# Attention and gated MLP on one core: the split of the attention output interleaved bank by bank, the second pair's split moved ahead of the weight steps, and ten weight blocks in the attention

## The chip, the core and the metric

The kernel runs on one core of a Trainium2 chip. A core has engines that run side by side, each taking its own instructions in order: TensorE (PE in the profile; its weight loads are shown apart as PEld), VectorE (DVE), ScalarE (ACT), GpSimd (POOL), and SyncE (SP), which here only issues transfers between the chip's memory and the core's on-chip memory, SBUF. TensorE writes its results to a small accumulator memory, PSUM, from which ScalarE and VectorE read them. The metric is the device time of one execution in microseconds (us), lower being better. An engine that needs another's result waits at a semaphore, and everything behind the waiting instruction on that engine waits with it.

## What is computed

Two stages, in fp32: attention with a sigmoid in place of the softmax over 12 heads, and a gated MLP over its output, with a normalisation and a mixing of positions in the gate. Cut to what matters:

```python
# q, k, v: (8, 12, 448, 64)
scores = q @ k.T / sqrt(64) - log(448)
x = concat_heads(sigmoid(scores) @ v)             # (8, 448, 768)
h = relu(x @ w_in)                                # w_in (768, 1024)
u, v = h[..., :512], h[..., 512:]
v_n = (v - mean(v)) / sqrt(var(v) + 1e-6)
v_s = einsum('ts,bsd->btd', w_spatial, v_n) + b_spatial
out = (u * v_s) @ w_out                           # w_out (512, 768)
```

## The kernel before, in words

**Products in three terms.** TensorE multiplies numbers in a rounded form (`F32R`). To keep fp32 accuracy, an operand is split into a high part (the rounded copy) and a low part (the operand less that copy); a product is the sum of high·high, low·high and high·low (`TERMS`). The helper `split` (L97 to L99) makes both parts: a copy on a chosen engine into the high part, then a `tensor_sub` on VectorE into the low part.

**Stages.** The eight batch entries go in four groups `m` of two. Each group has two stages. In the *attention* a loop runs over six pairs of units (`attention`, L484); a unit is two heads of one entry. Then come the *gate and output* products: `gate_values` (pv), `spatial` (pg), `gated` (pu) and `output` (po).

**One turn of the attention.** A turn writes seven score tiles psc (first the short one, L251, then the even unit's three and the odd unit's three, L269), ScalarE makes `at` from each with the sigmoid (L277), and TensorE multiplies them with v into `pav` (L295). `pav` is one tile of two PSUM banks: bank 0 for the even unit, bank 1 for the odd one. It is split into the two parts of `x_s`: ScalarE casts bank 0 and bank 1 (L305), then VectorE subtracts for bank 0 and bank 1 (L307). The very first turn takes its scores from the raw q and k; all later turns use `qks`, the split q and k. The cast of `qks` is ScalarE's in the first two entries, which are group 0 (`b > 1` in L237 otherwise), and VectorE's later.

**PSUM.** All PSUM tiles come from one ring of four buffers of two banks each (`banks`, tag ps2). One turn takes eight: the short tile, three even, three odd, and `pav`. So the fourth tile of a turn, psc of t = 2, stands in the buffer of the previous turn's `pav` and has to wait until all four reads of it are done; and a turn's `pav` stands in the buffer of its own psc of t = 2, and has to wait until ScalarE has made `at` from that.

**Weights.** w_in, w_spatial and w_out come from memory in 22 blocks and are split on the way by the generator `weight_steps`, which is advanced by `load_weights`. The first `NFIRST` = 11 blocks (the v half of w_in, w_spatial, and one block of the u half) take three advances each, or one for w_spatial, on VectorE alone, during group 0's attention: `weigh` spends `NYIELDS` = 25 of them there, four in a turn and five in the last. The other 11 take two advances each, with part of the work on ScalarE, during group 0's gate stage; a block's parts are spread over three rounds (`begin`; `middle`; the subtraction).

**What sets the order.** Each engine runs its instructions in the order in which the code issues them (`in_program_order`); the framework puts in the semaphore waits. It treats the reads of one PSUM tile by two engines as dependent: the later reader waits for the earlier.

Of the kernel before, what the change touches and what calls it, by code (L numbers as in the profile page):

```python
# [8 lines left out]
F32 = mybir.dt.float32  # L9
# [26 lines left out]
def attn_gmlp_kernel(  # L36
# [25 lines left out]
    nc = tc.nc  # L62
    B, NHP, _, _ = qk.shape
    S = out.shape[3]
    D = P // 2
    NCC = out.shape[1]
    DM = NCC * P
    F = w_in.shape[1] // (4 * NCC)
    NFC = F // P
# [18 lines left out]
    x_s = const.tile([P, 2, NCC, 2 * S], F32R, name="x_s")  # L88
# [8 lines left out]
    def split(hi, lo, src, copy):  # L97
        copy(hi, src)  # L98
        nc.vector.tensor_sub(lo, src, hi.bitcast(F32))  # L99

    def banks(name):
        return ps_2.tile([P, 2, 512], F32, tag="ps2", name=name)


    WEIGH = 4
# [22 lines left out]
    def weight_steps():  # L128
# [8 lines left out]
        def load(n):  # L137
            if n < len(steps):
                src, _, i = steps[n]
                w = 512 if src is w_sp else 1024  # L140

                if n < NFIRST:
                    raw = work.tile([P, 1024], U32, tag="tmp", name=f"wraw_{n}", bufs=3)[:, :w]
                else:
                    raw = work.tile([P, 1024], U32, tag="raw", name=f"wraw_{n}", bufs=4)
                raws[n] = raw.bitcast(F32) if src is w_sp else raw
                nc.sync.dma_start(raws[n], src[:, i * w : (i + 1) * w])
# [10 lines left out]

        for n, (src, dst, i) in enumerate(steps[:NFIRST]):
            load(n + AHEAD)  # L160
# [35 lines left out]
        begun, joined = {}, {}  # L196
        for n in range(NFIRST, len(steps) + 2):
            load(n + AHEAD)
# [8 lines left out]
            yield  # L207


    NFIRST = NCC + NFC + 1  # L210
    NYIELDS = 3 * (NCC + 1) + NFC

    weights = weight_steps()

    def load_weights(n):
        for _ in range(n):
            next(weights, None)
# [16 lines left out]
    def attention_splits(b, hp):  # L234
        raw = loaded[b, hp][:, :PART]
        s = work.tile([P, 2, 2 * S], F32R, tag="split", name=f"qks_{b}_{hp}", bufs=3)[:, :, :PART]
        split(s[:, 0], s[:, 1], raw, nc.vector.tensor_copy if b > 1 else nc.scalar.copy)  # L237
        parts_of[b, hp] = s
# [5 lines left out]
    def attention_scores(b, hp, t):  # L244
        psc = banks(f"psc_{b}_{hp}_{t}")
        if t == NFULL:
            for odd in range(2):
                raw = loaded[b, hp + odd]
                for j in range(2):
                    rows = slice(j * D, (j + 1) * D)  # L250
                    nc.tensor.matmul(  # L251
                        psc[odd * HALF : (odd + 1) * HALF, j, :S],
                        raw[rows, PART:],
                        raw[rows, FULL:PART],
                        start=True,
                        stop=True,
                    )
        else:
            unit = b, hp + t // (NFULL + 1)
            k = t % (NFULL + 1) * P  # L260
            if unit in parts_of:
                s = parts_of[unit]
                ops = [(s[:, a], s[:, e]) for a, e in TERMS]
            else:
                ops = [(loaded[unit], loaded[unit])]
            for i, (st, mv) in enumerate(ops):
                for j in range(2):
                    rows = slice(j * D, (j + 1) * D)
                    nc.tensor.matmul(  # L269
                        psc[:, j, :S],  # L270
                        st[rows, k : k + P],
                        mv[rows, FULL:PART],
                        start=i == 0,
                        stop=i == len(ops) - 1,
                    )
        at = work.tile([P, 2, 512], F32, tag="big", name=f"at_{b}_{hp}_{t}", bufs=BIG)[:, :, :S]
        nc.scalar.activation(at, psc[:, :, :S], AF.Sigmoid, bias=bias_s, scale=QK)  # L277
        return at

    def attention_values(b, hp, ats):  # L280
        vt = values[b, hp]
        pav = banks(f"pav_{b}_{hp}")
        evens, odds = range(NFULL), range(NFULL + 1, TILES)
        for t in (*evens, *odds, NFULL):
            at = ats(t)
            for odd in range(2):
                if t == NFULL:
                    rows = slice(odd * HALF, (odd + 1) * HALF)
                elif (t > NFULL) == odd:
                    rows = slice(0, P)  # L290
                else:
                    continue
                for j in range(2):
                    heads = slice(j * D, (j + 1) * D)
                    nc.tensor.matmul(  # L295
                        pav[heads, odd, :S],
                        vt[rows, t, heads],
                        at[rows, j],
                        start=t == odd * (NFULL + 1),
                        stop=t == NFULL,  # L300
                    )
        cols = slice((b % 2) * S, (b % 2 + 1) * S)
        parts = [(x_s[:, :, hp + odd, cols], pav[:, odd, :S]) for odd in range(2)]
        for x, ps in parts:
            nc.scalar.copy(x[:, 0], ps)  # L305
        for x, ps in parts:
            nc.vector.tensor_sub(x[:, 1], ps, x[:, 0].bitcast(F32))  # L307

    def product(ps, pairs, more=(), start=True, stop=True):

        ops = [(st(a), mv(c)) for st, mv in pairs for a, c in TERMS] + list(more)
        for i, (st, mv) in enumerate(ops):
            nc.tensor.matmul(ps, st, mv, start=start and i == 0, stop=stop and i == len(ops) - 1)  # L313
# [10 lines left out]
    def half_of(w, o, k, n):  # L324

        block, col = divmod((o // 2 * n + k) * 2 + o % 2, 4)
        return w[:, block, :, col * P : (col + 1) * P]
# [84 lines left out]
    def gated(b, fcs, copy=nc.scalar.copy):  # L412

        odd = b % 2
        g = gates.pop((b, fcs))
        pu = banks(f"pu_{b}_{fcs[0]}")
        for i, fc in enumerate(fcs):
            fs = slice(fc * P, (fc + 1) * P)
            product(
                pu[:, i, :S],  # L420
                [
                    (
                        lambda a, cc=cc: half_of(w_in_s, fc, cc, NCC)[:, a],
                        lambda c, cc=cc: x_s[:, c, cc, odd * S : (odd + 1) * S],
                    )
                    for cc in range(NCC)
                ],
            )
        load_weights(2)
        nc.vector.scalar_tensor_tensor(g, pu[:, :, :S], 0.0, g, op0=ALU.max, op1=ALU.mult)  # L430
        gs = work.tile([P, 2, 2 * S], F32R, tag="split", name=f"gs_{b}_{fcs[0]}", bufs=3)
        gs = gs.rearrange("p a (i s) -> p a i s", i=2)
        split(gs[:, 0], gs[:, 1], g, copy)
        for i, fc in enumerate(fcs):
            hidden[b, fc] = gs[:, :, i]
        load_weights(1)

    def output(b, es, parts=1, final=False):

# [32 lines left out]
    def ahead(f, n, end=len(units)):  # L472
        if n < end:
            f(*units[n])
# [9 lines left out]
    def attention(m):  # L484

        first, end = 2 * NHP * m, 2 * NHP * (m + 1)
        ats = {}
        budget = [NYIELDS if m == 0 else 0]

        def weigh(n):  # L490
            n = min(n, budget[0])
            budget[0] -= n
            load_weights(n)

        def scores(n, ts):
            for t in ts:
                ats[n, t] = attention_scores(*units[n], t)

        short, evens, odds = (NFULL,), tuple(range(NFULL)), tuple(range(NFULL + 1, TILES))
        for n in range(first, end, 2):  # L500
            if n:
                scores(n, short + evens)
            else:
                scores(n, evens)

            def loads():
                ahead(value_loads, n + 2, end)
                ahead(attention_loads, n + 4, end)
                ahead(attention_loads, n + 5, end)

            if n and n == first:
                yield
                attention_splits(*units[n + 1])
            if n:
                loads()
            scores(n, odds)
            if not n:
                scores(n, short)
            weigh(WEIGH + (n + 2 == end))
            if not n:  # L520
                loads()
            ahead(attention_splits, n + 2, end)
            ahead(attention_splits, n + 3, end)
            attention_values(*units[n], lambda t: ats.pop((n, t)))

    start_loads(0)
    load_weights(1)
    warm_up()
    pairs = [(0, 1), (2, 3)]
    running = attention(0)  # L530
    for m in range(B // 2):
        for _ in running:
# [80 lines left out]
```

## Time and profile before

| what | value |
|---|---|
| median of three runs | 690.48 us (690.3 to 690.51) |
| the profiled execution's own time | 690.91 us |
| its span, first to last instruction | 689.1 us |
| PE busy | 677.9 us, 98% |
| DVE busy | 280.6 us, 41% |
| ACT busy | 245.8 us, 36% |
| granted TensorE clock | 1.000 |

The span is 1.81 us shorter than the time of the execution it comes from. The page gives busy time by engine and the costliest groups of instructions; the chain of work that ended last follows the end of the program back to its start, at each step to what released it; the waits list who sat idle for whom; the timeline lists single instructions in order of time. A busy PE is not a PE at its peak, since the ends of matmuls are modelled.

### The profile page before, as it was taken

To read this page: it belongs to the slowest core of one execution; us is meant where nothing else is said; L and a number is where in the kernel's file an instruction comes from. 1 tells how busy PE (TensorE), PEld (TensorE's weight loads), DVE (VectorE), ACT (ScalarE), POOL (GpSimd) and SP (SyncE) were. 2 spreads that over 40 slices of the span, in tenths; PEclk is the share of its full clock that TensorE was granted. 3 is DMA by queue.
4 is the path that set the end of the run, shared out by engine and by line. 5 is a ranking of instruction groups with operands and counts; after the bars stand their busy time and mean duration, and the time that the engine had idled before them with its cause. 6 is when DMAs were issued, how large, how long until landed. Compare 5 with 4: busy or idle time off the path is not lost.

```text
span 689.1 us, 9062 instructions
## 1 busy us (share of the span) xinstructions
PE 677.9 (98%) x3826; PEld 508.2 (74%) x3826; DVE 280.6 (41%) x447; ACT 245.8 (36%) x303; POOL 18.5 (3%) x36
## 2 busy tenths in 40 slices
PE   8999999999999999999999999999999999999997
PEld 3545789998655488999864558899985546889996
DVE  3868688823234037222242414621233421653020
ACT  6777322313467510011356741011136664101111
POOL 0000010000000001000000001100000000110000
PEclk9999999999999999999999999999999999999999
DMA  6854113060433000005062200000515410000102
GB/s 235 321 183 156 49 44 95 28 214 25 166 131 107 1 1 0 1 28 186 28 212 88 104 1 0 1 1 27 187 54 187 138 51 1 0 1 0 54 28 80
DMA packets 20553, 55.37 MB, mean 80 GB/s; under 512 B 1953, under 2 KB 8353, under 8 KB 20513
## 3 DMA queue, kind: packets, MB, share of 16 engines
q1 hardware_dynamic: 20224, 54.57, 22.7%
q8 instruction: 30, 0.49, 0.3%
q10 hardware_dynamic: 288, 0.23, 0.1%
q14 instruction: 11, 0.08, 0.0%
HBM read 43.78 MB, written 11.01 MB: 80 GB/s over the span
## 4 chain that ended last, share of the span: by engine, by line
PE 92%; DVE 4%; ACT 3%; issue 1%
PE pav L295 20%; PE pu L313 17%; PE po L313 17%; PE pv L313 17%; PE pg L313 10%; PE psc L269 10%; DVE x_s L307 3%; ACT x_s L305 3%; PE psc L251 1%; PE warm L322 0%; DVE qks L99 0%; DVE gs L99 0%; DVE g L430 0%; DVE osb L463 0%; ACT osb L461 0%
## 5 line engine op out<-in xcount | busy, mean ns | idle before, releaser
L277 ACT ACTIVATE at<-psc,bias_s 128x896 f32<-128x896 f32 x168 | 154.3, 1032 | 23.0 <-PE psc L251 18.6
L295 PE MATMUL pav<-at,v 128*64 128x448 f32 (+1 forms) x768 | 135.4, 548 | 0.0
L313 PE MATMUL po<-gs,w_out_s 128*128 128x448 f32 x576 | 120.4, 368 | 1.0 <-DVE osb L463 0.9
L313 PE MATMUL pu<-x_s,w_in_s 128*128 128x448 f32 x576 | 118.0, 365 | 0.0
L313 PEld LDWEIGHTS po<-gs,w_out_s 128*128 128x128 f32 x576 | 107.7, 188 | 12.6 <-DVE osb L463 1.2
L313 PE MATMUL pv<-w_in_s,x_s 128*128 128x512 f32 x504 | 115.5, 390 | 0.0
L313 PEld LDWEIGHTS pu<-x_s,w_in_s 128*128 128x128 f32 x576 | 108.2, 188 | 8.5
L313 PEld LDWEIGHTS pv<-w_in_s,x_s 128*128 128x128 f32 x504 | 94.3, 188 | 22.3 <-issue 2.8
L295 PEld LDWEIGHTS pav<-at,v 128*64 128x64 f32 (+1 forms) x768 | 44.2, 135 | 80.5 <-issue 73.3
L269 PE MATMUL psc<-qks 64*128 64x448 f32 x828 | 96.8, 374 | 5.6 <-DVE x_s L307 4.6
L269 PEld LDWEIGHTS psc<-qks 64*128 64x128 f32 x828 | 77.8, 184 | 31.9 <-PE psc L269 11.6
L307 DVE TENSOR_TENSOR x_s<-pav,x_s 128x448 fp32r<-128x448 f32 x48 | 27.8, 620 | 135.8 <-ACT x_s L305 135.8
L313 PE MATMUL pg<-w_sp_s,vn 128*128 128x448 f32 x352 | 72.8, 365 | 0.0
L313 PEld LDWEIGHTS pg<-w_sp_s,vn 128*128 128x128 f32 x352 | 66.0, 187 | 5.8
L467 ACT COPY osb<-po 128x896 f32<-128x896 f32 x23 | 20.9, 908 | 114.9 <-PE po L313 104.6
L430 DVE SCALAR_TENSOR_TENSOR g<-pu,g 128x896 f32<-128x896 f32 x16 | 17.5, 1091 | 82.5 <-PE pu L313 82.5
L98 DVE CAST qks<-raw 128x832 fp32r<-128x832 f32 x36 | 21.2, 588 | 72.1 <-DMA raw<-qk_dram 36.9
L305 ACT CAST x_s<-pav 128x448 fp32r<-128x448 f32 x48 | 23.2, 536 | 76.0 <-PE pav L295 76.0
L99 DVE TENSOR_TENSOR qks<-raw,qks 128x832 fp32r<-128x832 f32 x46 | 46.7, 1025 | 4.5 <-ACT qks L98 1.4
L98 ACT CAST gs<-g 128x896 fp32r<-128x896 f32 x12 | 11.3, 943 | 100.7 <-DVE g L430 100.7
L348 ACT ACTIVATE rv<-pv 128x1024 f32<-128x1024 f32 (+1 forms) x16 | 14.7, 916 | 76.0 <-PE pv L313 74.3
L352 DVE BATCH_NORM_STATS2 stats<-rv 128x6 f32<-128x512 f32 x28 | 19.0, 679 | 39.5 <-ACT rv L348 39.5
(42 smaller groups left out, 242.5 us busy)
## 6 DMA issues: line engine op xcount, KB each, us to landing
raw<-qk_dram SPq DMA_DIRECT2D x48, 448.0 KB, 5.3
v<-v_dram SPq DMA_DIRECT2D x24, 448.0 KB, 3.4
out_dram<-osb SPq DMA_DIRECT2D x23, 448.0 KB, 2.6
wraw<-w_in_dram SPq DMA_DIRECT2D x12, 512.0 KB, 5.8
wraw<-w_out_dram SPq DMA_DIRECT2D x6, 512.0 KB, 3.6
wraw<-w_sp_dram SPq DMA_DIRECT2D x4, 256.0 KB, 5.1
b_bc<-b_sp_dram SPq DMA_DIRECT2D x1, 256.0 KB, 5.0
out_dram<-osb ACTq DMA_DIRECT2D x2, 112.0 KB, 1.7
```

The source lines that it names most:

```text
L98: copy(hi, src)
L99: nc.vector.tensor_sub(lo, src, hi.bitcast(F32))
L269: nc.tensor.matmul(psc[:, j, :S], st[rows, k : k + P], mv[rows, FULL:PART], start=i == 0, stop=i == len(ops) - 1,)
L277: nc.scalar.activation(at, psc[:, :, :S], AF.Sigmoid, bias=bias_s, scale=QK)
L295: nc.tensor.matmul(pav[heads, odd, :S], vt[rows, t, heads], at[rows, j], start=t == odd * (NFULL + 1), stop=t == NFULL,)
L305: nc.scalar.copy(x[:, 0], ps)
L307: nc.vector.tensor_sub(x[:, 1], ps, x[:, 0].bitcast(F32))
L313: nc.tensor.matmul(ps, st, mv, start=start and i == 0, stop=stop and i == len(ops) - 1)
L348: nc.scalar.activation(rv[:, :n], pv[:, :n], AF.Relu)
L352: nc.vector.bn_stats(stats, rv[:, i])
L430: nc.vector.scalar_tensor_tensor(g, pu[:, :, :S], 0.0, g, op0=ALU.max, op1=ALU.mult)
L467: nc.scalar.copy(osb, po[:, :, :S])
```

## The change

Three edits. In `attention_values` the loop "both casts, then both subtractions" becomes a loop over the banks that calls `split`, so that the subtraction of bank 0 stands between the two casts. In the first turn (`n` = 0) the transfers of later turns and the splits of the second pair's q and k stand ahead of the weight steps, and one weight advance is made there instead of four. And `NFIRST` is 10 instead of 11, with 22 advances in the attention instead of 25; the block that leaves (the first of the u half) is prepared in group 0's gate stage, where `gated` makes two advances at its end instead of one.

```diff
-    NFIRST = NCC + NFC + 1
-    NYIELDS = 3 * (NCC + 1) + NFC
+    NFIRST = NCC + NFC
+    NYIELDS = 3 * NCC + NFC
...
-        parts = [(x_s[:, :, hp + odd, cols], pav[:, odd, :S]) for odd in range(2)]
-        for x, ps in parts:
-            nc.scalar.copy(x[:, 0], ps)
-        for x, ps in parts:
-            nc.vector.tensor_sub(x[:, 1], ps, x[:, 0].bitcast(F32))
+        for odd in range(2):
+            x, ps = x_s[:, :, hp + odd, cols], pav[:, odd, :S]
+            split(x[:, 0], x[:, 1], ps, nc.scalar.copy)
...
-        load_weights(1)
+        load_weights(2)
...
-            weigh(WEIGH + (n + 2 == end))
-            if not n:
+            if n:
+                weigh(WEIGH + (n + 2 == end))
+            else:
                 loads()
             ahead(attention_splits, n + 2, end)
             ahead(attention_splits, n + 3, end)
+            if not n:
+                weigh(1)
             attention_values(*units[n], lambda t: ats.pop((n, t)))
```

What this does to the instructions is shown at three places. The first is ScalarE between the first and the second turn: the casts of the second pair's q and k (`qks_2`, `qks_3`), the two casts of `pav`, and the first sigmoid of the next turn. In brackets stand the engines whose semaphores are waited for. Before:

```order
L98 CAST qks_2_156<-raw_2_81 128x832 [waits DMAHW3_49]
L98 CAST qks_3_159<-raw_3_83 128x832 [waits DMAHW4_49]
L305 CAST x_s<-pav_0_162 128x448 [waits PE_49]
L305 CAST x_s<-pav_0_162 128x448
L277 ACTIVATE at_2_3_188<-psc_2_3_183,bias_s 128x2x448 [waits PE_49,Activation_49]
```

After the change, the same rows:

```order
L98 CAST qks_2_141<-raw_2_81 128x832 [waits DMAHW3_49]
L98 CAST qks_3_144<-raw_3_83 128x832 [waits DMAHW4_49]
L98 CAST x_s<-pav_0_153 128x448 [waits PE_49]
L98 CAST x_s<-pav_0_153 128x448 [waits DVE_49]
L277 ACTIVATE at_2_3_179<-psc_2_3_174,bias_s 128x2x448 [waits PE_49,Activation_49]
```

The order is the same, but the second cast now has a wait for VectorE. It is counted so that it ends with the subtraction of bank 0. The same row stands in each of the 24 turns.

The second place is the start of VectorE's program: the first weight block (`wval`, `wraw`, `w_in_s`), the first w_spatial block, the second pair's q and k, and the first `pav`. Before:

```order
L116 TENSOR_SCALAR wval_137<-wraw_85 128x512 [waits DMAHW5_49]
L169 TENSOR_SCALAR wraw_85<-wraw_85 128x512 [waits DVE_49]
L173 TENSOR_SCALAR wraw_85<-wraw_85 128x512 [waits DVE_49]
L119 SCALAR_TENSOR_TENSOR wval_137<-wraw_85,wval_137 128x512 [waits DVE_49]
L122 SCALAR_TENSOR_TENSOR wval_137<-wraw_85,wval_137 128x512 [waits DVE_49]
L178 CAST w_in_s<-wval_137 128x512 [waits DVE_49]
L179 TENSOR_TENSOR w_in_s<-wval_137,w_in_s 128x512 [waits DVE_49]
L178 CAST w_sp_s<-wraw_87 128x512 [waits DMAHW6_49]
L179 TENSOR_TENSOR w_sp_s<-wraw_87,w_sp_s 128x512 [waits DVE_49]
L99 TENSOR_TENSOR qks_2_156<-raw_2_81,qks_2_156 128x832 [waits DMAHW3_49,Activation_49]
L99 TENSOR_TENSOR qks_3_159<-raw_3_83,qks_3_159 128x832 [waits DMAHW4_49,Activation_49]
L307 TENSOR_TENSOR x_s<-pav_0_162,x_s 128x448 [waits PE_49,Activation_49]
```

After the change:

```order
L99 TENSOR_TENSOR qks_2_141<-raw_2_81,qks_2_141 128x832 [waits DMAHW3_49,Activation_49]
L99 TENSOR_TENSOR qks_3_144<-raw_3_83,qks_3_144 128x832 [waits DMAHW4_49,Activation_49]
L116 TENSOR_SCALAR wval_149<-wraw_85 128x512 [waits DMAHW5_49]
L169 TENSOR_SCALAR wraw_85<-wraw_85 128x512 [waits DVE_49]
L173 TENSOR_SCALAR wraw_85<-wraw_85 128x512 [waits DVE_49]
L99 TENSOR_TENSOR x_s<-pav_0_153,x_s 128x448 [waits Activation_49] x2
L119 SCALAR_TENSOR_TENSOR wval_149<-wraw_85,wval_149 128x512 [waits DVE_49]
L122 SCALAR_TENSOR_TENSOR wval_149<-wraw_85,wval_149 128x512 [waits DVE_49]
L178 CAST w_in_s<-wval_149 128x512 [waits DVE_49]
L179 TENSOR_TENSOR w_in_s<-wval_149,w_in_s 128x512 [waits DVE_49]
L178 CAST w_sp_s<-wraw_87 128x512 [waits DMAHW6_49]
L179 TENSOR_TENSOR w_sp_s<-wraw_87,w_sp_s 128x512 [waits DVE_49]
```

The subtractions for q and k and those for `pav` have moved ahead of most of the first weight block; both subtractions for `pav` now wait for ScalarE, where one wait stood ahead of the two. On SP's queue the transfers of the next pair's v, q and k move with them, ahead of the third weight block's.

The third place is VectorE in group 0's gate stage, from the weight advances behind `gs_0` to the subtraction of `gs_2`, the second operand of the output product. Before:

```order
L119 SCALAR_TENSOR_TENSOR wval_1029<-wraw_946,wval_1029 128x512
L122 SCALAR_TENSOR_TENSOR wval_1029<-wraw_946,wval_1029 128x512 [waits DVE_49]
L116 TENSOR_SCALAR wval_1127<-wraw_1027 128x512 [waits DMAHW7_49]
L187 TENSOR_SCALAR wraw_1027<-wraw_1027 128x512 [waits DVE_49]
L203 TENSOR_TENSOR w_out_s<-wval_1029,w_out_s 128x512 [waits Activation_49]
L119 SCALAR_TENSOR_TENSOR wval_1078<-wraw_992,wval_1078 128x512
L122 SCALAR_TENSOR_TENSOR wval_1078<-wraw_992,wval_1078 128x512 [waits DVE_49]
L430 SCALAR_TENSOR_TENSOR g_2_1034<-pu_2_1090,g_2_1034 128x2x448 [waits PE_49]
L99 TENSOR_TENSOR gs_2_1136<-g_2_1034,gs_2_1136 128x896 [waits Activation_49]
```

After the change:

```order
L119 SCALAR_TENSOR_TENSOR wval_1019<-wraw_936,wval_1019 128x512
L122 SCALAR_TENSOR_TENSOR wval_1019<-wraw_936,wval_1019 128x512 [waits DVE_49]
L116 TENSOR_SCALAR wval_1082<-wraw_1017 128x512 [waits DMAHW6_49]
L187 TENSOR_SCALAR wraw_1017<-wraw_1017 128x512 [waits DVE_49]
L203 TENSOR_TENSOR w_out_s<-wval_1019,w_out_s 128x512 [waits Activation_49]
L119 SCALAR_TENSOR_TENSOR wval_1068<-wraw_982,wval_1068 128x512
L122 SCALAR_TENSOR_TENSOR wval_1068<-wraw_982,wval_1068 128x512 [waits DVE_49]
L116 TENSOR_SCALAR wval_1127<-wraw_1066 128x512 [waits DMAHW7_49]
L187 TENSOR_SCALAR wraw_1066<-wraw_1066 128x512 [waits DVE_49]
L203 TENSOR_TENSOR w_out_s<-wval_1068,w_out_s 128x512 [waits Activation_49]
L428 SCALAR_TENSOR_TENSOR g_2_1024<-pu_2_1087,g_2_1024 128x2x448 [waits PE_49]
L99 TENSOR_TENSOR gs_2_1133<-g_2_1024,gs_2_1133 128x896 [waits Activation_49]
```

One weight advance of three instructions (L116, L187, L203) stands ahead of `g_2` and `gs_2` that stood behind them before.

## The prediction

> **What bounds the kernel now.** I read the page first: it says which engine fills the span and what the chain of work that ended last consists of.
>
> ```profile
> span 689.1 us, 9062 instructions
> ...
> PE 677.9 (98%) x3826; PEld 508.2 (74%) x3826; DVE 280.6 (41%) x447; ACT 245.8 (36%) x303; POOL 18.5 (3%) x36
> ...
> PE 92%; DVE 4%; ACT 3%; issue 1%
> ```
>
> PE is the bound nearly everywhere, and the change removes no matmul. What can move is the part of the chain that is not PE. The chain in order of time says where that lies: between the turns of the attention. The columns are start, length, and what. The first two such places:
>
> ```profile
> 15.47 0.02 issue
> 15.50 0.98 ACT x_s L305 x2
> 16.48 1.95 DVE qks L99 x2
> 18.43 1.08 DVE x_s L307 x2
> 19.51 0.14 issue
> 19.64 2.71 PE psc L269 x23
> 22.35 5.62 PE pav L295 x32
> 27.97 0.02 issue
> 27.99 0.98 ACT x_s L305 x2
> 28.97 0.02 issue
> 28.99 1.17 DVE x_s L307 x2
> 30.16 0.14 issue
> 30.29 2.71 PE psc L269 x24
> 33.00 5.62 PE pav L295 x32
> ```
>
> From the end of one pav to the start of the next it takes 33.00 − 27.97 = 5.03 us, and in the first place 22.35 − 15.47 = 6.88 us. There are 5 such places in each of the 4 groups (6 turns), 20 in all, one of them the first. In all, psc of t = 2 starts when both subtractions have freed pav's buffer, 30.29 − 27.97 = 2.32 us after the end of pav. PE is busy with the short tile and psc of t = 0 and 1 meanwhile, so that little of this is idle time; the waits say how much (total, times, longest):
>
> ```profile
> PE psc L269 <- DVE x_s L307: 4.6, 20, 0.8
> ```
>
> The longest is the first place; the others have (4.6 − 0.8)/19 = 0.20 each. So 0.20 us per place is all that a quicker release could win, and a release that comes later is paid in full.
>
> **The interleaved split.** The group of the subtractions (instruction, count, busy us, mean ns of one, idle time before), then single instructions from the timeline: the casts and the sigmoids behind them, and a place where ScalarE waits for VectorE:
>
> ```profile
> L307 DVE TENSOR_TENSOR x_s<-pav,x_s 128x448 fp32r<-128x448 f32 x48 | 27.8, 620 | 135.8 <-ACT x_s L305 135.8
> ```
>
> ```profile
> 197.38 0.97 ACT L305 CAST x_s<-pav 128x448 fp32r<-128x448 f32 x2 [3.38 <-PE pav L295]
> 197.81 0.54 ACT L305 CAST x_s<-pav 128x448 fp32r<-128x448 f32 x1
> 198.24 1.03 ACT L277 ACTIVATE at<-psc,bias_s 128x896 f32<-128x896 f32 x1
> 200.92 1.93 ACT L277 ACTIVATE at<-psc,bias_s 128x896 f32<-128x896 f32 x2
> 292.45 1.09 DVE L430 SCALAR_TENSOR_TENSOR g<-pu,g 128x896 f32<-128x896 f32 x1 [4.10 <-PE pu L313]
> 293.58 0.95 ACT L98 CAST gs<-g 128x896 fp32r<-128x896 f32 x1 [6.35 <-DVE g L430]
> ```
>
> Neighbours on one engine overlap: a cast lasts 0.54, but the next instruction starts 0.43 behind its start (197.38, 197.81, 198.24), and the two subtractions together last 1.17, not 2 × 0.62. A hand-over breaks this overlap. Before there is one, after the change three: cast 0, subtraction 0, cast 1, subtraction 1, since the rows of the program show the second cast waiting for the first subtraction. A hand-over from ACT to DVE costs 0.02 (28.97 above); from DVE to ACT 293.58 − 293.54 = 0.04. Counted from the end of pav: cast 0 from 0.02 to 0.56, subtraction 0 from 0.58 to 1.20, cast 1 from 1.24 to 1.78, subtraction 1 from 1.80 to 2.42, and with the 0.14 of the chain PE goes on at 2.56 instead of 2.32: 0.24 later.
>
> Behind the waiting cast on ScalarE stand the seven sigmoids of the next turn. In the rows above the first of them starts 0.86 after the first cast, or 0.88 after the end of pav. After the change it starts 0.43 behind cast 1, at 1.67: 0.79 later. The fourth sigmoid, of psc t = 2, starts (200.92 − 198.24) = 2.68 later, at 4.35, and lasts 1.03: it ends at 5.38. The next pav stands in that buffer and cannot start earlier. Before, the same sum is 0.88 + 2.68 + 1.03 = 4.59, below the 5.03 at which PE came to pav, so ScalarE hid behind PE by 0.44. Now PE would come at 2.56 + 2.71 = 5.27, and ScalarE's release comes later. **ScalarE takes over as what ends last.** Its hand-over to PE does not show in the trace of before; the nearest rows are DVE's to PE, 0.14 above and, at the end of the program, 0.04:
>
> ```profile
> 682.51 0.40 DVE osb L463
> 682.91 0.04 issue
> 682.96 2.74 PE po L313 x12
> ```
>
> I take 0.14, of the same ring in the same turn, as the value: pav at 5.52, that is 0.49 later than now at each place. With 0.04 it is 0.39; were ScalarE not in the way, PE alone gives 0.24. All of this repeats, since each turn waits for the one before: 19 places × 0.49 = **+9.3 us** (with 0.04: 7.4; PE alone: 4.6).
>
> **The second pair's split ahead.** In the first place the two subtractions of q and k (1.95 us) stand ahead of those of pav because VectorE ran the first weight blocks until 16.48. Now they come first:
>
> ```profile
> 11.48 1.71 ACT L98 CAST qks<-raw 128x832 fp32r<-128x832 f32 x2
> ...
> 12.89 0.69 DVE L119 SCALAR_TENSOR_TENSOR wval<-wraw,wval 128x512 uint32<-128x512 uint32 x1
> ```
>
> ```profile
> L99 DVE TENSOR_TENSOR qks<-raw,qks 128x832 fp32r<-128x832 f32 x46 | 46.7, 1025 | 4.5 <-ACT qks L98 1.4
> 11.48 0.43 DVE L116 TENSOR_SCALAR wval<-wraw 128x512 uint32<-128x512 uint32 x1 [10.30 <-DMA wraw<-w_in_dram]
> ```
>
> ScalarE's casts end at 13.19; the second subtraction ends about 13.19 + 0.02 + 1.03 = 14.24; the one weight advance ahead of pav's subtractions takes 12.89 − 11.48 = 1.41 and ends about 15.65. The first of them is due at 15.47 + 0.58 = 16.05, so nothing holds it. The first place becomes like the others, 5.52 instead of 6.88: **−1.4 us** (at 0.04: −1.5; PE alone: −1.6). The transfers that SP issues earlier (the next v, q and k) land well ahead of their use a turn later; the third weight block's, now behind them, has a turn as well, since its first step moves from the second turn's start to its end. In the later turns of group 0 VectorE must be free when the first cast ends:
>
> ```profile
> 36.06 1.96 DVE L99 TENSOR_TENSOR qks<-raw,qks 128x832 fp32r<-128x832 f32 x2 [0.95 <-DMA wraw<-w_sp_dram]
> 39.64 1.16 DVE L307 TENSOR_TENSOR x_s<-pav,x_s 128x448 fp32r<-128x448 f32 x2 [1.62 <-ACT x_s L305]
> ```
>
> It idles 1.62 there. ScalarE's casts of q and k come 0.79 later, the pav 0.49 later, and the first subtraction is wanted 0.43 earlier: 1.62 − 0.79 + 0.49 − 0.43 = 0.89 is left. Cost nothing; were it used up, the excess would be paid at 4 places.
>
> **Ten blocks.** The attention of group 0 gives one block away; VectorE was not what PE waited for there, so this wins nothing. In the gate stage the first 17 advances have the same content for a block earlier; one more stands ahead of gs_2:
>
> ```profile
> 127.77 1.08 DVE L430 SCALAR_TENSOR_TENSOR g<-pu,g 128x896 f32<-128x896 f32 x1
> 129.87 1.09 DVE L99 TENSOR_TENSOR gs<-g,gs 128x896 fp32r<-128x896 f32 x1 [1.01 <-ACT gs L98]
> 130.88 0.42 DVE L116 TENSOR_SCALAR wval<-wraw 128x512 uint32<-128x512 uint32 x1
> ...
> 132.28 0.68 DVE L119 SCALAR_TENSOR_TENSOR wval<-wraw,wval 128x512 uint32<-128x512 uint32 x1
> ```
>
> ```profile
> 131.78 14.78 PE po L313 x72
> ```
>
> VectorE is behind here, so gs_2 moves by the whole advance, 132.28 − 130.88 = 1.40, from an end at 130.96 to 132.36. The output product uses its low part first in the ninth matmul, 131.78 + 8 × 14.78/72 = 133.42. Cover left: 1.06 us; cost nothing, and at most a few tenths if VectorE is later than that, once in the program.
>
> **The sum** against the profiled execution (690.91, span 689.1): +9.3 − 1.4 = +7.9, a span of 697.0 and a time of 698.8. That execution lies 0.43 above the median, so for the median 690.48 + 7.9 = **698.4 us**, 1.1% slower. The bounds from the hand-over: 690.48 + 7.4 − 1.5 = 696.4, and somewhat above 698.4 if each of the three hand-overs costs up to 0.05 more on this path (19 × 2 × 0.05 = 1.9 for the two ahead of the sigmoids): 700.3.
>
> **Rivals.**
>
> *The second cast does not in effect wait* (faster). If bank 1 could be cast while bank 0 is subtracted, cast 1 would run at 0.45 as now, subtraction 1 would end at 0.58 + 1.17 = 1.75, and PE would find the buffer free when it comes, 0.20 earlier than now, 2.12; pav at 2.12 + 2.71 = 4.83, behind ScalarE's 4.59 + 0.14 = 4.73. That is 19 × −0.20 and 4.83 − 6.88 = −2.05 in the first place: −5.9, or 684.6 us. It decides from the point where the wait's target is done before cast 0 ends. Against it: the wait stands in the program in all 24 turns, and its target cannot start before cast 0 ends. Chance 0.06. [...]
>
> *PE alone sets the new turn*: the sigmoids run closer together than now, or pav is not held by the fourth of them. Then the place takes 5.27, 0.24 more: 4.6 − 1.6 = +3.0, or 693.5 us. For it: the trace never shows PE waiting for a sigmoid. Against it: the pitch of the sigmoids is the same in all rows, and the ring's arithmetic is fixed. Chance 0.07.
>
> *VectorE's cover is used up*: gs_2 or the q and k of group 0 are late by more than 1 us, some 1 to 2 us over the forecast: about 700 us. Chance 0.04.
>
> *The gain and the loss cancel*, within 0.2% (1.4 us, about what a measurement of this kernel can tell from no change): it needs a loss of about 0.1 per place, less than half of what PE alone gives. Chance 0.03.
>
> **How the numbers follow.** The forecast (696.4 to 700.3) has 0.80. The range, 694.2 to 700.0, leaves out the faster case, the even one, PE alone's middle and the top of the forecast, under 0.2 together. Slower by over 0.2%: 0.80 + 0.07 + 0.04 = 0.91; within 0.03; faster 0.06.
>
> **What would show it.** In the waits of the changed kernel: ACT's x_s waiting for DVE's x_s 24 times, some 0.7 each; PE's psc waiting 0.43 for x_s at 20 places; a new wait of pav for the sigmoids, about 0.25 at 20 places. In the chain: 5.5 us from the end of pav to the next, the first place like the rest; the gate stages with their lengths of before (28.8, 9.08, 14.6). Wrong would be: pav starting as soon as psc ends (PE alone), casts that follow at 0.43 (no wait), or idle PE in front of the output product.

## The result, and the profile after

The changed kernel takes 699.0 us (median of four runs, 698.39 to 699.13) against 690.5 us before (690.3 to 691.2): a ratio of 1.012, interval 1.0102 to 1.0137. The prediction was 698.4 us, with 694.2 to 700.0 as its range. The profiled execution has a span of 697.2 us, 8.1 more than before.

The page of the changed kernel, the rows that answer to those of before:

```profile
span 697.2 us, 9039 instructions
...
PE 681.9 (98%) x3826; PEld 505.9 (73%) x3826; DVE 281.6 (40%) x445; ACT 249.1 (36%) x305; POOL 18.5 (3%) x36
...
PE 91%; DVE 4%; ACT 3%; issue 1%; DMA 0%
```

The matmuls are the same 3826. The block that left the attention takes two instructions from VectorE to ScalarE. The busy times of PE, VectorE and ScalarE rise by 1.0 to 4.0 us, and nothing on the page says where the 8.1 us go. The chain in order of time shows it (start, length, what), here from the first pav to the second:

```profile
15.96 0.02 issue
15.98 0.54 ACT x_s L98
16.52 0.02 issue
16.55 0.64 DVE x_s L99
17.18 0.02 issue
17.21 0.54 ACT x_s L98
17.75 0.02 issue
17.77 0.64 DVE x_s L99
18.41 0.14 issue
18.54 2.83 PE psc L269 x23
21.37 0.03 issue
21.39 5.69 PE pav L295 x32
```

Where one cast row and one subtraction row stood, there are four links with three hand-overs. The place takes 21.39 − 15.96 = 5.43 us, where the first place took 6.88 before and all others 5.03. The subtractions of q and k are gone from the chain.

The waits of the changed kernel (total, times, longest):

```profile
PEld pav L295 <- ACT at L277: 18.8, 66, 0.4
ACT x_s L98 <- DVE x_s L99: 16.6, 24, 0.7
PE psc L269 <- DVE x_s L99: 9.1, 20, 0.5
```

The middle row is the new wait, once in each of 24 turns, 0.69 us each. The last has grown from 4.6. The first is what PE's weight loads for pav wait for the sigmoids, 6.7 us in 23 waits before; many of these waits are hidden behind running matmuls, so the row is no measure of the loss (e10 below, the fastest kernel, has 18.2). The timeline, in a later group, shows the one that is not hidden (start, length, engine, instruction, idle time before and its releaser):

```profile
200.12 0.53 ACT L98 CAST x_s<-pav 128x448 fp32r<-128x448 f32 x1 [0.69 <-DVE x_s L99]
200.54 6.40 ACT L277 ACTIVATE at<-psc,bias_s 128x896 f32<-128x896 f32 x7
204.31 0.20 PEld L295 LDWEIGHTS pav<-at,v 128*64 128x64 f32 x4 [0.39 <-ACT at L277]
```

Before, the first weight loads for pav at the same place waited for no sigmoid:

```profile
202.35 0.20 PEld L295 LDWEIGHTS pav<-at,v 128*64 128x64 f32 x4 [0.31 <-issue]
```

With the pitch and length that the sigmoids had before, the fourth of the seven starts 2.68 behind 200.54 and ends 1.03 later, at 204.25; pav starts at 204.31, which is 5.44 after the end of the previous pav. The release by VectorE alone would have let pav start at 2.58 + 2.71 = 5.29. PE's own row shows no idle time for the difference: the chain counts it into psc, 2.83 to 2.85 us long instead of 2.71, and a matmul's end is modelled.

From the start of one pav to the start of the next it is 11.05 to 11.13 us at all 20 places, against 10.64 to 10.69 at 19 places and 12.49 at the first before. From the last pav of a group to the first of the next it is 116.22 to 116.24, before 116.15 to 116.17: the gate and output stages are unchanged within 0.1 us.

### The profile page after: what moved, and what is told of

It reads as the page before. It is cut to its first block, busy times and chain, and to the rows that moved or that the text cites. A ratio compares the mean times of both kernels' runs of the same rounds, so it can differ in the third digit from the quotient of the medians.

```text
span 697.2 us, 9039 instructions
## 1 busy us (share of the span) xinstructions
PE 681.9 (98%) x3826; PEld 505.9 (73%) x3826; DVE 281.6 (40%) x445; ACT 249.1 (36%) x305; POOL 18.5 (3%) x36
## 4 chain that ended last, share of the span: by engine, by line
PE 91%; DVE 4%; ACT 3%; issue 1%; DMA 0%
PE pav L295 20%; PE pu L311 17%; PE po L311 17%; PE pv L311 17%; PE psc L269 11%; PE pg L311 10%; DVE x_s L99 4%; ACT x_s L98 3%; PE psc L251 1%; DMA raw<-qk_dram 0%; DVE gs L99 0%; DVE g L428 0%; DVE osb L461 0%; ACT osb L459 0%; DVE gs L98 0%
## 5 line engine op out<-in xcount | busy, mean ns | idle before, releaser
L269 PE MATMUL psc<-qks 64*128 64x448 f32 x828 | 99.1, 378 | 9.1 <-DVE x_s L99 9.1
L269 PEld LDWEIGHTS psc<-qks 64*128 64x128 f32 x828 | 75.4, 184 | 40.2 <-PE psc L269 16.1
L99 DVE TENSOR_TENSOR x_s<-pav,x_s 128x448 fp32r<-128x448 f32 x48 | 30.0, 625 | 142.4 <-ACT x_s L98 142.4
L98 ACT CAST x_s<-pav 128x448 fp32r<-128x448 f32 x48 | 25.6, 532 | 86.2 <-PE pav L295 69.6
```

What stands on the lines that cost most here:

```text
L269: nc.tensor.matmul(psc[:, j, :S], st[rows, k : k + P], mv[rows, FULL:PART], start=i == 0, stop=i == len(ops) - 1,)
```

## The experiments

Eleven kernels ran. "Turn" is the time from the start of one pav to the next in that kernel's profile, first places apart. The times of before are those measured on the same chip.

**One part of the change at a time.** e1 has the interleaving alone:

```diff
-        parts = [(x_s[:, :, hp + odd, cols], pav[:, odd, :S]) for odd in range(2)]
-        for x, ps in parts:
-            nc.scalar.copy(x[:, 0], ps)
-        for x, ps in parts:
-            nc.vector.tensor_sub(x[:, 1], ps, x[:, 0].bitcast(F32))
+        for odd in range(2):
+            x, ps = x_s[:, :, hp + odd, cols], pav[:, odd, :S]
+            split(x[:, 0], x[:, 1], ps, nc.scalar.copy)
```

> The kernel before with the interleaved split as its only edit. Theory (the second cast waits for the first subtraction, which delays the next turn's sigmoids by 0.79 and, through the fourth of them, the next pav): 0.48 us more at each of 19 places, and about 0.9 more at the first place, where the subtractions stand behind q's and k's: +10, about 700.5 us; ScalarE's x_s waiting for VectorE 24 times. Rival A (the front or the ten blocks cost the time, the interleaving is hidden): 690.5 within 1 us. Rival B (PE alone, by the later release): 0.24 at 20 places, about 695.3.

Measured: 700.76 us against 690.77, ratio 1.0139 (1.0123 to 1.0154); a turn of 11.05 to 11.13. The interleaving alone makes the whole loss and more; rivals A and B fall.

e2 is the changed kernel with these lines put back, so that the front and the ten blocks remain.

> The changed kernel with both casts ahead of both subtractions again; the front and the ten blocks stay. Theory: the 20 places take 5.03 us each, the first one too (6.88 before): -1.85, about 688.7 us, the gate stages as long as before. Rival A: 698 to 699, or anything above 690.5, from the gate stage of the first group or from its attention.

Measured: 690.04 us against 690.77, ratio 0.9986 (0.9977 to 0.9994); turns of 10.63 to 10.69, the first included. It is a gain, but of 0.7 us rather than 1.85. The starts of the first two pav in its chain show a part of the reason:

```profile
10.32 5.62 PE pav L295 x32
20.95 5.62 PE pav L295 x32
```

The second pav is 22.35 − 20.95 = 1.40 earlier than before, not 1.85, since the first is 0.46 later than in the profile of before (9.86). That start is not the change's: over the profiles of all kernels it lies between 10.23 and 10.97 with the front of the change and between 9.86 and 11.19 without it (see the last section). Before, the second pav was set by VectorE, which starts with the arrival of the first weight block (at 11.48, after 10.3 us of waiting for it), so that a late start of TensorE was absorbed: in e3, which keeps the front of before, the first pav starts at 11.14 and the second at 22.79, a first place of 11.65 rather than 12.49. The change moves this place onto PE's chain and gives up that cushion. The times point the same way: the eleven runs of e2 spread over 1.62 us, the 21 of before over 0.69. How the 1.40 of the profile becomes 0.7 in the medians was not followed further. Together with the interleaving the front is worth more: e1 loses 9.99 us and the changed kernel 8.5, though on different chips. In e1 the second pav starts at 23.07, later than before, since VectorE is late there (q's and k's subtractions end at 18.31, before at 18.43) and the longer split stands behind it (1.77 to 20.08, before 1.08 to 19.51).

e3 has the ten blocks alone:

```diff
-    NFIRST = NCC + NFC + 1
-    NYIELDS = 3 * (NCC + 1) + NFC
+    NFIRST = NCC + NFC
+    NYIELDS = 3 * NCC + NFC
...
-        load_weights(1)
+        load_weights(2)
```

> The kernel before with ten blocks in the attention and two advances at the end of gated, and nothing else. Theory: no effect, 690.5 within 0.5 us; the output product of the first group starts without a wait, and gs_2 is done about 1 us ahead of its use. Rival (VectorE is late in the gate stage): PE waits ahead of the first output product, some 0.5 to 2 us more.

Measured: 690.82 us against 690.77, ratio 0.9999 (0.999 to 1.0008). The output product of group 0 starts at 132.23 right behind the spatial one, and gs_2 is done at 132.81, 1.06 ahead of its first use at 132.23 + 1.64. No effect, as expected.

**What of the interleaving costs the time.** e5 delays ScalarE alone, in the kernel before, and leaves the split of pav as it is:

```diff
+        if t == NFULL and (b, hp) != (0, 0):
+            nc.scalar.activation(at[:, :, :320], psc[:, :, :320], AF.Sigmoid, bias=bias_s, scale=QK)
         nc.scalar.activation(at, psc[:, :, :S], AF.Sigmoid, bias=bias_s, scale=QK)
```

> The kernel before, with ScalarE alone made later: an extra sigmoid of 640 of the 896 columns ahead of each turn's first one, some 0.8 us, in place of the 0.79 that the change adds there. The split of pav and its release stay as they are. Theory (the fourth sigmoid of a turn frees the buffer of its pav and has taken over): pav at 0.88 + 0.81 + 2.68 + 1.03 + 0.06 = 5.46 instead of 5.03 at 19 places, +8, about 699 us, with PE waiting ahead of pav and not ahead of psc. Rival (PE alone, by the release of pav): no effect, 690.8.

Measured: 701.04 us against 690.99, ratio 1.0148 (1.0131 to 1.0165); a turn of 11.10 to 11.17. The waits of e5:

```profile
PE psc L269 <- DVE x_s L309: 4.6, 20, 0.8
```

and a part of its chain:

```profile
199.75 0.98 ACT x_s L307 x2
...
202.06 2.23 PE psc L269 x16
204.28 0.03 issue
204.31 0.87 PE psc L269 x6
205.18 0.03 issue
205.21 5.69 PE pav L297 x32
```

The wait for pav's release is what it was, 4.6 in all, and yet a turn is as long as in the changed kernel. The delay of the sigmoids is enough for the whole loss; PE alone, which gave no effect here, falls. The turn is 0.02 to 0.09 longer than worked out (5.62 + 5.46 = 11.08): the sigmoids start 0.84 later, not 0.81, pav takes 5.69, and the last score tile waits for a sigmoid too, so that it and pav start 0.90 apart instead of 2.70/4 = 0.68.

e6 was to delay the release alone:

```diff
-        for x, ps in parts:
+        for odd, (x, ps) in enumerate(parts):
             nc.vector.tensor_sub(x[:, 1], ps, x[:, 0].bitcast(F32))
+            if not odd:
+                nc.vector.tensor_sub(x[:, 1, :96], ps[:, :96], x[:, 0, :96].bitcast(F32))
```

> The kernel before, with the release of pav alone made later: 96 columns of the first subtraction are done a second time between the two subtractions, some 0.25 us; the sigmoids are not delayed. Both theories: psc of t = 2 starts 0.25 later and all of it is paid at 20 places: +5, about 695.8 us. That is the part of the interleaving's cost that the later release would have made alone (0.24 a place); with e5 at about +8 the two delays do not add up to more than the larger of them in the change (0.48 a place).

Measured: 684.8 us against 690.99, ratio 0.9912 (0.9897 to 0.9927): faster, a turn of 10.27 to 10.36 but for 10.55 at the first place and 10.56 at the last, with more work. In its timeline PE runs through the scores without a wait:

```profile
195.85 4.02 PE L269 MATMUL psc<-qks 64*128 64x448 f32 x36
```

The program tells why. The framework does not assign PSUM buffers in a fixed ring, as the prediction took for granted; how it chooses no run shows, but the longer split alone changed the choice. With the four buffers called A to D, the tiles of the second and third turn (short, t = 0, 1, 2, 4, 5, 6, pav; the pav before them in A):

```text
before  D C B A D C B A    D C B A D C B A
e6      D C B D A C B D    A C B A D C B A
```

In e6 the tile t = 2 stands in the short tile's buffer, which the first sigmoid frees, and the previous pav's buffer goes to t = 4, which comes later. So e6 did not test the release, and its expectation failed; whether the buffers alone make the 6.2 us, e11 tells. The changed kernel, e1 to e5 and e7 have the buffers of before for every PSUM tile, so that no comparison among them is one of buffers, and the prediction's ring held where it was used.

e7 is the changed kernel with its order kept and the second cast on VectorE, so that ScalarE waits for no subtraction:

```diff
-            split(x[:, 0], x[:, 1], ps, nc.scalar.copy)
+            split(x[:, 0], x[:, 1], ps, nc.vector.tensor_copy if odd else nc.scalar.copy)
```

> The changed kernel, its interleaved order kept, with the second cast on VectorE instead of ScalarE: cast 0, subtraction 0, cast 1, subtraction 1, with one hand-over and no wait on ScalarE. Theory (the wait of the second cast costs the time, not the order): release at about 0.56 + 0.02 + 0.54 + 0.50 + 0.03 + 0.62 + 0.14 = 2.41 instead of 2.32, sigmoids earlier than before: 0.05 to 0.1 a place above the run without the interleaving, 691 to 692 us. Rival (the order by banks itself is slow): 698 to 699.

Measured: 694.01 us against 690.99, ratio 1.0047 (1.0032 to 1.0062); a turn of 10.86 to 10.88. That lies between the expectation and its rival: per turn the order by banks without the waiting cast costs about half as much. Its chain and its waits:

```profile
197.87 0.62 DVE x_s L99
198.49 0.54 DVE x_s L98
199.03 0.02 issue
199.06 0.64 DVE x_s L99
199.69 0.14 issue
199.83 2.71 PE psc L269 x23
```

```profile
PE psc L269 <- DVE x_s L99: 8.5, 20, 0.4
```

The release comes at 199.69 − 197.28 = 2.41 after the end of pav, where the expectation had 2.27 without the hand-over: the second subtraction starts at 199.06 − 197.28 = 1.78 instead of 1.65, since the first subtraction holds VectorE for 0.62 and the cast for 0.54, where I had taken 0.54 and 0.50. PE waits 8.5/20 = 0.42 per turn instead of 0.20, and the turn is 0.22 longer: a later release is paid in full. That is the size which the prediction gave to "PE alone" (0.24), here with ScalarE out of the way.

e8 gives each bank of pav a PSUM tile of its own, so that the program has no wait between cast and subtraction:

```diff
-        pav = banks(f"pav_{b}_{hp}")
+        pav = [ps_2.tile([P, 512], F32, tag="ps1", name=f"pav_{b}_{hp}_{odd}", bufs=2) for odd in range(2)]
```

with `bufs=3` for the common ring and `pav[odd]` in place of `pav[:, odd]` at its uses.

> The changed kernel with pav as two PSUM tiles of one bank each, in a ring of their own, so that the second cast waits for no subtraction; the common ring has three buffers left instead of four. Theory: the second cast starts 0.43 behind the first, while the first subtraction runs, and both have their usual lengths; the split ends about 1.75 after the end of pav instead of 2.42. The ring of three makes the scores wait for the sigmoids, each tile for the third before it: 4.65 + 0.68 = 5.33 from pav to pav, so about 10.95 a turn, above the 10.65 without the interleaving and below the changed kernel's 11.12. If the wait were not what delays the second cast, it would still start 1.2 behind the first and a turn take above 11.1. What the ring of three does to the gate stages is not forecast.

Measured once: 702.49 us, a turn of 11.10 to 11.12 at 19 of 20 places and one of 11.38. Its timeline:

```profile
201.96 0.97 ACT L98 CAST x_s<-pav 128x448 fp32r<-128x448 f32 x2 [3.84 <-PE pav L295]
202.53 1.16 DVE L99 TENSOR_TENSOR x_s<-pav,x_s 128x448 fp32r<-128x448 f32 x2 [6.83 <-ACT x_s L98]
```

The two casts follow each other in 0.97 again, the first subtraction starts while the second cast runs, and the split ends at 203.69, 1.75 after the end of pav (201.94), to the hundredth the number of the rival that had no wait. So it is the wait that lengthens the split, and not the order. From 202.53 to 202.93, for 0.40 us, the two engines read the two tiles at once, and the pairs last 0.97 and 1.16, as in the kernel before (0.97 at 197.38, 1.16 at 39.64). The time itself says nothing on this, since the ring of three holds the scores to the pace of the sigmoids (in its chain they start at 204.18, 205.07, 205.97 and 206.87, and the sigmoids are (4.60 − 1.01)/4 = 0.90 apart), more than the 10.95 that I worked out; what a turn would take without the wait and with four buffers was not measured.

e9 assigns the buffers in the changed kernel by hand as e6 had them, with four tags of one buffer each (`bufs=1`):

```diff
+    slots = [0, 1, 2, 3]
+
-    def banks(name):
-        return ps_2.tile([P, 2, 512], F32, tag="ps2", name=name)
+    def banks(name, at=0):
+        slots.append(slots.pop(at))
+        return ps_2.tile([P, 2, 512], F32, tag=f"ps2_{slots[-1]}", name=name)
...
-        psc = banks(f"psc_{b}_{hp}_{t}")
+        psc = banks(f"psc_{b}_{hp}_{t}", at=int(t == 2 and (b % 2, hp) != (0, 0)))
```

> The changed kernel with the PSUM buffers assigned by hand: in each turn after a group's first, psc of t = 2 stands in the buffer of the turn's short tile, and psc of t = 4 in that of the previous pav. PE then waits for no subtraction ahead of t = 2. Theory (ScalarE's sigmoids, delayed by the waiting cast, set the turn): the release by VectorE does not matter, the fourth sigmoid still frees pav's buffer at 5.44 after the end of pav, a turn stays at 11.1 and the time at 698 to 699. Rival (PE alone, by the release of pav): the turn falls to 10.3 to 10.65, the time to 684 to 690.

Measured: 698.8 us against 691.15, ratio 1.0111 (1.0094 to 1.0128); a turn of 11.09 to 11.16. The waits and the timeline of e9:

```profile
PE psc L272 <- ACT at L280: 12.3, 20, 0.6
```

```profile
191.11 2.73 PE L272 MATMUL psc<-qks 64*128 64x448 f32 x24 [0.61 <-ACT at L280]
```

PE has no wait for a subtraction left, and nothing is won: it now waits for the first sigmoid ahead of t = 2. The expectation had overlooked this wait. In its chain:

```profile
190.05 1.02 ACT at L280
191.07 0.04 issue
```

The end of this sigmoid is 2.69 after the end of pav (188.38, 0.02 ahead of the first cast), later than VectorE released PE in the changed kernel (2.58). So e9 shows that the loss stands when PE waits for ScalarE alone, but it put a new wait in the place of the old one and does not by itself tell the two theories apart. Against e11 below, with the same buffers and the split of before, its turn is 0.78 longer, 0.61 of it this wait. What tells them apart is e5, where the delay of ScalarE alone makes the whole loss, with e7, where the late release alone makes half, and the timeline of the changed kernel, where pav starts 0.06 behind the fourth sigmoid.

**Better than both.** e4 takes both banks in one instruction on each engine, on top of the change's other parts:

```diff
-        for odd in range(2):
-            x, ps = x_s[:, :, hp + odd, cols], pav[:, odd, :S]
-            split(x[:, 0], x[:, 1], ps, nc.scalar.copy)
+        x, ps = x_s[:, :, hp : hp + 2, cols], pav[:, :, :S]
+        split(x[:, 0], x[:, 1], ps, nc.scalar.copy)
```

> The changed kernel with one cast of both banks on ScalarE and one subtraction of both on VectorE, in place of two and two: one hand-over. Theory: cast 0.94, subtraction 1.09, release at 0.02 + 0.94 + 0.02 + 1.09 + 0.14 = 2.21 after the end of pav instead of 2.32, sigmoids not delayed: 0.11 less than before at 19 places and 1.96 less at the first: -4, about 686.5 us, below both kernels. If a release that comes earlier wins nothing (the sigmoids or the issue set the turn): as without the interleaving, 688.7.

Measured: 685.52 us against 690.77, ratio 0.9921 (0.9908 to 0.9933); a turn of 10.42 to 10.48, about 0.21 less than before instead of 0.11: in its waits PE's matmuls no longer wait for the subtraction at all.

e10 adds e9's buffers to e4, e11 puts them into the kernel before and changes nothing else.

> The run with one cast and one subtraction for both banks, and these buffers as well. Theory: PE neither waits for a subtraction nor loads weights anew behind such a wait, a turn takes 10.33 as in e6 instead of 10.43: about 683.5 us. If e6's turn came from its repeated subtraction and not from the buffers: 685.5 as without them.

> The kernel before with these buffers and nothing else. If e6 was fast because the framework gave t = 2 another buffer, a turn takes 10.33 here too and the time is about 685 us; the first place stays as long as before, VectorE being late there. If e6 was fast by its repeated subtraction: 690.8.

Measured: e10 682.5 us against 691.15, ratio 0.9877 (0.9863 to 0.9892), turns of 10.23 to 10.35; e11 684.44 us, ratio 0.9903 (0.9889 to 0.9918), turns of 10.27 to 10.36 but for the last at 10.58. So e6 was fast by its buffers. The chains of e4 and e10 differ in one thing, the scores between two pav (short tile, then 36 records of the others):

```profile
194.89 0.75 PE psc L251 x8
195.65 4.15 PE psc L269 x36
```

```profile
26.11 0.75 PE psc L254 x8
26.86 3.91 PE psc L272 x36
```

Neither chain has a link on another engine there, but e4's scores still take 0.24 longer (its pav is 0.07 shorter): its weight loads wait for the split, 7.2/20 = 0.36 a turn, a wait that e10 does not have:

```profile
PEld psc L269 <- DVE x_s L99: 7.2, 20, 0.4
```
e10 is the fastest of the kernels that ran, 1.2% below the kernel before.

## Why the prediction was right, point by point

**The wait of the second cast** was right in kind and size. Forecast from the end of pav: release of the buffer with its hand-over at 2.56; in the profile 18.54 − 15.96 = 2.58. The wait is there 24 times at 0.69, and PE's wait for the release is 9.1/20 = 0.46 a place, forecast 0.43.

**ScalarE takes over** was right. e5 gives the whole loss by a delay of ScalarE alone, and e7 half of it when only the release is late (0.22 a turn, forecast 0.24); e9 agrees, without deciding it. The new wait of pav was forecast at 0.25 a place and is smaller, 5.44 − 5.29 = 0.15, because of the next point.

**The hand-over from ScalarE to PE** was the unknown of the sum, taken at 0.14 from VectorE's row. It is 0.06 (204.25 to 204.31). From the end of pav to the next this gave 5.43 to 5.44 instead of the 5.52 of the forecast. Most turns still came out at 11.12 to 11.13 for a forecast of 5.62 + 5.52 = 11.14, because the chain has pav itself at 5.69 instead of 5.62 when PE had to wait ahead of it; the first turn of each group, which begins with a pav that PE did not wait for (5.62), takes 11.05. Over the 19 places 211.15 − 202.39 = 8.8 us were lost for a forecast of 9.3. That it is so close is partly luck: two errors of 0.08 and 0.07 nearly cancelled.

**The split ahead** was right as a step, −1.45 for the first place in the profile (6.88 to 5.43; forecast −1.4), and VectorE had room: it idles 0.39 us ahead of the first subtraction of pav there. But the step was sized from one execution with an early start. Without the interleaving it is worth 0.7 us (e2), not the 1.85 expected there, for it takes away the cushion that absorbed a late start of TensorE. In the changed kernel's profile that start is 10.34 − 9.86 = 0.48 later, which the forecast did not have. The span adds up: 8.8 at the 19 places, −1.45 at the first, 0.48 at the start, and 0.3 in the gate and output stages and behind the last pav make 8.1. Without the late start it is 7.6, for a forecast of 7.9.

**Ten blocks** cost nothing, as forecast: gs_2 ends at 133.38 in

```profile
132.29 1.09 DVE L99 TENSOR_TENSOR gs<-g,gs 128x896 fp32r<-128x896 f32 x1 [1.01 <-ACT gs L98]
```

```profile
132.80 14.78 PE po L311 x72
```

which is 1.40 later against the output product than before, and 1.06 ahead of its first use at 134.44: both numbers of the forecast.

**The rivals.** "The second cast does not in effect wait" fell with the wait's row, and its arithmetic (a split of 1.75) was borne out by e8, where the wait was gone. "PE alone" fell by e5 and the timeline. "VectorE's cover is used up" fell by e3 for gs_2, and for q and k by the turns of group 0, which are as long as the others. "The gain and the loss cancel" fell by the result. What none of them had is that the buffers are the framework's choice, which a slightly longer instruction can change.

## What to carry to other kernels

Before interleaving by buffer halves, ask whether the halves are independent to whoever places the waits; that it pays when they are, no run here shows. In these programs two engines reading one tile are put in sequence, so work that ran back to back on each engine becomes a chain with a hand-over at every link (2.43 us here from the first cast to the end of the last subtraction, instead of 2.17), and everything queued behind the new wait moves with it. Before judging a release, ask which of two releases ends last; a delay of one engine that was hidden by 0.44 us cost 0.48 a turn once it was 0.79 late. And look at which buffer a tile stands in: handing the buffer that comes free late to the tile that is needed late won more (e11, 1%) than any reordering here.

## What was not expected of the hardware

TensorE starts at about half its later pace in e3, and the moment of the change differs between the profiles, while every profile has a mean granted clock of 0.999 or 1.000. In the first score tiles of e3 the weight loads come in pairs; a pair takes 0.34 us and the next follows 0.74 behind, until 7.06, and then 0.19 and 0.37 (timeline of PEld):

```profile
6.32 0.34 PEld L269 LDWEIGHTS psc<-raw 64*128 64x128 f32 x2 [0.41 <-issue]
7.06 0.19 PEld L269 LDWEIGHTS psc<-raw 64*128 64x128 f32 x2 [0.39 <-issue]
```

In the changed kernel the shorter loads begin at 5.51, over the thirteen profiles here between 4.65 (before) and 7.11 (e6). The later they begin, the later the first pav starts, from 9.86 (before) to 11.19 us (e6), a spread of more than the 0.7 us that the front is worth in e2. What sets the moment was not shown: the six matmuls that run ahead of these tiles are the same in every kernel.
